# GpSimd's constants and half batch 1's decay rows issued earlier, and the planner's keys reset, in a fused forgetting attention and gated FFN

## The chip, the cores and the metric

The kernel runs on one core of a Trainium2 chip. A time is the device time of one execution in microseconds (us); lower is better. Before the change the median of five runs is 271.87 us (271.43 to 272.63). The profile is one execution, taken by the hardware profiler. Its engines are PE (TensorE matmul), PEld (TensorE weight load), DVE (VectorE), ACT (ScalarE), POOL (GpSimd) and SP (SyncE, which here only issues DMAs). A name with a q (SPq) is the queue of that engine.

## The reference

Eight batches, eight heads, 576 positions, head dimension 64. Attention has a decay: the logs of the forget gates f are summed along the sequence, and the difference of the sums is added to the scaled score. The outcome, eight heads side by side, is the input of an FFN: a matmul to 1024 channels, ReLU, a convolution over three neighbouring positions, a sigmoid gate, and a matmul back to 512.

```python
cum = cumsum(log(clip(f, 1e-4, 1)), -1)
s = q @ k.T / 8 + cum[..., :, None] - cum[..., None, :]      # causal
x = softmax(s) @ v                                            # heads side by side: (8, 576, 512)
h = maximum(x @ w_in, 0)
c = cw[0] * h[t - 1] + cw[1] * h[t] + cw[2] * h[t + 1]        # zero outside the sequence
out = (h * sigmoid(c)) @ w_out
```

## The kernel before

**Attention.** The work goes in 16 half batches `hb` of four heads, each in two pairs `i` of two heads. q and k of a half batch come by transposing DMAs on SP's queue (`load_qk`, L110) as 16-bit halves of their fp32 numbers into `stq` and `stk`, 128 rows by 4 x 576 columns, in a ring of four buffers each. Of the rows that hold low halves, some carry other things: rows 126 of `stq` and 96 and 98 of `stk` carry the decay sums as a high and a low bfloat16 part (`khi`, `klo`). Before use, DVE multiplies a buffer by a 0/1 column and adds another (`clamp`, L119), and POOL writes constant rows into it by DMA (`fill`, L132, from the tile `consts`, which DVE fills in L544 to L546). From half batch `CLAMPS` on, the query side has no DVE clamp, but a fill of 48 rows more. Decay rows come for half batch 0 from the small tiles `khi4` and `klo4` (`rows_first(p, eng)`, pair by pair, L125 to L127), for half batch 1 from `khi_sb` and `klo_sb` (`rows_of`, L140 to L142), and for the others from `kd`, a copy in DRAM that L253 and L254 write (L144, L146).

Scores of a pair are a diagonal part (L330 lays down the causal mask, L298 adds q and k), two off-diagonal parts (L298), and, once per half batch, the tail of 64 positions (L304). ACT takes their exp (L338, L324, L310). PV (`pv`, L356) multiplies with V, which five DMAs on SP load per half batch (L163; per whole batch from half batch `HALVES` on) and DVE casts to fp16 (L170 to L173). It writes the one PSUM tile `O`; `norm` (L367, L369, DVE) reads it, divides by the row sums into `xn` and so frees it for the next pair's PV. w_in is loaded by POOL in one DMA (L634), which waits for a DVE write behind the norm of pair 0.

**FFN.** When a batch's four pairs are normed, PE transposes `xn` (L393, L401), ACT or DVE copies it out (L411, L413), and L425 multiplies with w_in: 16 groups of four matmuls per batch. ACT does ReLU (L438), DVE the convolution in two instructions (L455, L457), ACT tanh (L467; sigmoid in the last batch, L465), DVE the gate (L475, L473), PE the last matmul (L487, L500), ACT or DVE the copy out (L511, L513), POOL or SP the store (L520, L522). The weights of the convolution are transposed and prepared once (L275 to L287).

**The order.** Each engine works through its instructions in order. Up to L269 the order is that of the text: clamps and decay sums of half batch 0 on DVE, a few matmuls to keep PE running (L241), the first loads, the constants. After that it is made by a planner: `task(engines, after, key, fn, ...)` notes a cost per engine, what comes ahead of it, and a key; `play` (L713) runs the tasks in a list schedule with these costs, where an engine that is free takes the ready task with the lowest key, and the instructions are issued in that order. `t_norm` is the norm, the clamps are tasks of the key `2 * hb - 3 + 0.2 * s`, `AHEAD` bounds how far scores may run ahead of the FFN, `busy` says when each engine is thought to be free first.

## Time and profile before

| | before |
|---|---|
| median of 5 runs | 271.87 us |
| profiled execution | 272.01 us |
| its span, first to last instruction | 270.1 us |
| mean granted TensorE clock | 0.974 |
| PE busy | 240.8 us, 89% |
| DVE busy | 226.3 us, 84% |
| ACT busy | 212.0 us, 79% |
| POOL busy | 59.1 us, 22% |
| DMA queue of SP | 32.00 MB, 70.1% of 16 engines' span |

Busy time is the time in which an instruction of the engine runs; issuing a DMA counts for POOL alone. In a line of the timeline or of the waits, the first two numbers are start and length in us; then come engine, line, operation, what is written and what is read; the bracket at the end tells how long the engine stood idle before, and what ended that. In the chain of waits each piece was released by the one above it, back from the end of the kernel. The time to landing of a DMA counts from its issue.

### The profile page before, as it was taken

The page shows a single profiled execution, that of the slowest core. Times are in us where ns is not written, and L with a number is a line of the kernel's source. Part 1 is how long each engine was busy: PE and PEld are TensorE (multiplying, and loading weights), DVE is VectorE, ACT ScalarE, POOL GpSimd, SP SyncE. Part 2 cuts the span into 40 slices and gives each one's busy share as a digit, 9 for nine tenths or more (in the row PEclk, how much of TensorE's full clock was granted, in tenths as well). Part 3 has the DMA queues.
Part 4 walks back from the last instruction along what each step waited for, and adds up shares of the span by engine and source line. Part 5 has one row for each costly group of instructions (what it writes and reads, how often), then busy time and mean ns, then how long its engine had stood idle before and what let it go on. Part 6 is the DMA issues. An engine that isn't in the chain of part 4 may idle for free.

```text
span 270.1 us, 6596 instructions
## 1 busy us (share of the span) xinstructions
PE 240.8 (89%) x2577; PEld 166.2 (62%) x2602; DVE 226.3 (84%) x401; ACT 212.0 (79%) x347; POOL 59.1 (22%) x124
## 2 busy tenths in 40 slices
PE   2966779876999999999999999999999999989990
PEld 1335646655777777676776677667776767654640
DVE  4864548999799999999989989999899999978751
ACT  5081738889879999989989899989999998577552
POOL 4391111821131240314315050404110100000000
PEclk9995979999999999999999999999999999999997
DMA  7999999999999999999999999999411201022015
GB/s 130 219 219 185 222 184 236 190 186 208 188 225 176 211 238 197 209 233 223 263 211 180 222 269 182 190 138 233 127 43 37 80 0 67 14 117 80 0 47 226
DMA packets 121284, 44.58 MB, mean 165 GB/s; under 512 B 115560, under 2 KB 116596, under 8 KB 121254
## 3 DMA queue, kind: packets, MB, share of 16 engines
q1 hardware_dynamic: 115088, 32.00, 70.1%
q0 software_dynamic: 5840, 12.01, 17.2%
q8 instruction: 20, 0.33, 0.6%
q10 hardware_dynamic: 326, 0.17, 0.4%
q14 instruction: 10, 0.08, 0.1%
HBM read 13.99 MB, written 9.58 MB: 87 GB/s over the span
## 4 chain that ended last, share of the span: by engine, by line
PE 65%; DMA 10%; SPq 8%; issue 5%; ACT 5%; DVE 4%; POOL 0%; ACTq 0%; POOLq 0%
PE mm L425 19%; PE mm L487 19%; PE sc L298 12%; PE O L356 8%; DMA stk<-in_k_dram 6%; SPq L110 6%; DMA vf<-in_v_dram 3%; SPq L163 2%; PE sc L330 2%; PE sc L500 2%; PE mm L393 2%; DVE u L457 1%; DMA out_dram<-ob 1%; ACT po L324 1%; ACT ht L438 1%
## 5 line engine op out<-in xcount | busy, mean ns | idle before, releaser
L425 PE MATMUL mm<-xt,w_in_f 128*128 128x288 f16 x512 | 80.0, 290 | 1.8 <-DVE xt L413 0.4
L298 PE MATMUL sc<-stq,stk 128*128 128x128 bf16 (+3 forms) x576 | 67.2, 242 | 7.5 <-ACT pm L338 4.0
L324 ACT ACTIVATE po<-sc 128x1024 f16<-128x1024 f32 x64 | 64.6, 1028 | 2.0 <-PE sc L298 1.5
L438 ACT ACTIVATE ht<-mm 128x288 f16<-128x288 f32 x128 | 52.0, 414 | 11.9 <-PE mm L425 10.8
L425 PEld LDWEIGHTS <-w_in_f 128*128 128x128 f16 x512 | 47.8, 99 | 18.8 <-issue 3.5
L487 PE MATMUL mm<-w_out_f,hg 128*128 128x512 f16 x248 | 58.4, 379 | 0.7 <-ACT xt L411 0.6
L298 PEld LDWEIGHTS <-stk 128*128 128x128 bf16 x576 | 42.4, 99 | 27.0 <-issue 8.1
L455 DVE SCALAR_TENSOR_TENSOR u<-ht,cwt 128x576 f32<-128x576 f16 x64 | 51.5, 812 | 5.5 <-ACT ht L438 4.7
L457 DVE SCALAR_TENSOR_TENSOR u<-ht,cwt,u 128x576 f32<-128x576 f16 x64 | 51.6, 812 | 0.5
L475 DVE SCALAR_TENSOR_TENSOR hg<-hg,ht 128x576 f16<-128x576 f16 x56 | 41.7, 752 | 4.1 <-ACT hg L467 3.7
L467 ACT ACTIVATE hg<-u,cwt 128x576 f16<-128x576 f32 x56 | 43.4, 780 | 1.4 <-DVE u L457 1.3
L338 ACT ACTIVATE pm<-sc 128x1024 f16<-128x1024 f32 x32 | 32.9, 1027 | 12.2 <-DVE consts L544 6.1
L487 PEld LDWEIGHTS <-hg 128*128 128x128 f16 x248 | 23.6, 98 | 24.2 <-issue 0.9
L356 PE MATMUL O<-va,po 128*128 128x65 f16 x640 | 37.1, 195 | 1.2 <-ACT po L324 1.0
L356 PE MATMUL O<-va,pm 128*128 128x65 f16 x256 | 31.6, 195 | 3.2 <-DVE xn L369 1.8
L356 PEld LDWEIGHTS <-po 128*128 128x128 f16 x640 | 31.1, 98 | 2.4 <-ACT po L324 1.8
L132 POOL DMA_DIRECT2D stq<-consts x23 | 12.9, 563 | 76.6 <-DMA stq<-in_q_dram 26.9
L356 PEld LDWEIGHTS <-pm 128*128 128x128 f16 x256 | 24.4, 99 | 6.0 <-DVE xn L369 2.7
L369 DVE TENSOR_TENSOR xn<-O,rc 128x640 f16<-128x640 f32 x32 | 26.4, 824 | 1.1
L511 ACT ACTIVATE ob<-mm 128x512 f32<-128x512 f32 x23 | 13.7, 598 | 11.0 <-PE mm L487 10.7
L330 PE MATMUL sc<-trib,identb 128*128 128x512 bf16 x39 | 15.0, 385 | 1.3 <-ACT po L324 1.3
L522 POOL DMA_DIRECT2D out_dram<-ob x10 | 7.5, 750 | 39.5 <-ACT ob L511 20.2
(112 smaller groups left out, 223.0 us busy)
## 6 DMA issues: line engine op xcount, KB each, us to landing
vf<-in_v_dram SPq DMA_DIRECT2D x64, 128.0 KB, 3.8
out_dram<-ob POOLq DMA_DIRECT2D x10, 512.0 KB, 5.4
out_dram<-ob SPq DMA_DIRECT2D x10, 256.0 KB, 2.1
stq<-consts POOLq DMA_DIRECT2D x8, 216.0 KB, 4.6
vf<-in_v_dram SPq DMA_DIRECT2D x16, 64.0 KB, 5.2
w_in_f<-in_moe_w_in_dram POOLq DMA_DIRECT2D x1, 1024.0 KB, 9.9
w_out_f<-in_moe_w_out_dram POOLq DMA_DIRECT2D x4, 256.0 KB, 6.1
out_dram<-ob SPq DMA_DIRECT2D x2, 512.0 KB, 2.8
```

The costliest lines, as they stand in the source:

```text
L298: nc.tensor.matmul(sc, stk_t[hb % RING][:, k0:k0 + 128], stq_t[hb % RING][:, q0:q0 + w], start=start, stop=stop, skip_group_check=True)
L324: nc.scalar.activation(p_of[i, s][:, 0:1024], sc_of.pop((i, s)), AF.Exp, scale=SCALE)
L338: nc.scalar.activation(p_of[i, 2], sc_of.pop((i, 2)), AF.Exp, scale=SCALE)
L356: nc.tensor.matmul(O[:, s, 65 * Q:65 * (Q + 1)], w, va[:, h, m, :], start=(m == 0), stop=(m == Q))
L369: nc.vector.tensor_tensor(xo, Ov[:, :, :, 0:64], rc.unsqueeze(3).broadcast_to((128, 2, NKB, 64)), op=ALU.mult)
L425: nc.tensor.matmul(ps[:, 0:w], w_in_f16[:, cc, 128 * ff:128 * (ff + 1)], xt[:, cc, w * t:w * (t + 1)], start=(cc == 0), stop=(cc == NCC - 1))
L438: nc.scalar.activation(ht[:, 0, HT_0 + w * t:HT_0 + w * (t + 1)], ps[:, 0:w], AF.Relu)
L455: nc.vector.scalar_tensor_tensor(u, hl, cwt[:, ff, 0:1], hc, op0=ALU.mult, op1=ALU.add)
L457: nc.vector.scalar_tensor_tensor(u, hr, cwt[:, ff, 1:2], u, op0=ALU.mult, op1=ALU.add)
L467: nc.scalar.activation(hv, u, AF.Tanh, scale=cwt[:, ff, 2:3])
L475: nc.vector.scalar_tensor_tensor(hv, hv, 1.0, hc, op0=ALU.add, op1=ALU.mult)
L487: nc.tensor.matmul(ps, chunk(g, ff, c), w_out_f16[:, ff, :], start=(ff == 0), stop=(ff == NFF - 1))
```

## The change

The memsets of POOL (ones and zeros around V and around the hidden tile, and the identity) stand before the loads of half batch 1's q and k in the text, and so ahead of POOL's first row DMAs. The rows of both pairs of half batch 0 are issued on ACT's queue. Half batch 1's rows are two tasks: the query row with the query transposes as its condition, the key rows with those of the keys. The copies to `kd` are a task behind them, on which the rows of the later half batches depend. Beside that, numbers of the planner are different: `CLAMPS` 6 in place of 8, `HALVES` 8 in place of 16, `AHEAD` 5.0 in place of 3.0, POOL's first free time, the keys of casts, norms, the second convolution and the copies out, and a few costs. The instructions of the program are as many as before on PE; on DVE two query clamps fewer.

```diff
@@ -119,12 +119,12 @@
         nc.vector.tensor_scalar(t, t, lim[0:p1, 2 * side:2 * side + 1], lim[0:p1, 2 * side + 1:2 * side + 2],
                                 op0=ALU.mult, op1=ALU.add)
 
-    def rows_first(p, eng):
+    def rows_first(p):
 
         tq, tk, c, r = stq_t[0], stk_t[0], slice(2 * p * S, 2 * (p + 1) * S), slice(64 * p, 64 * (p + 1))
-        eng.dma_start(tq[126:127, c], khi4[r, :])
-        eng.dma_start(tk[96:97, c], khi4[r, :])
-        eng.dma_start(tk[98:99, c], klo4[r, :])
+        nc.scalar.dma_start(tq[126:127, c], khi4[r, :])
+        nc.scalar.dma_start(tk[96:97, c], khi4[r, :])
+        nc.scalar.dma_start(tk[98:99, c], klo4[r, :])
 
     def fill(t, p0, n, z):
 
@@ -132,16 +132,18 @@
         nc.gpsimd.dma_start(bass.AP(tensor=t.tensor, offset=int(t.offset) + p0 * row, ap=[[2 * row, n], [1, HS]]),
                             consts[z:z + n, :])
 
+    def row_q(hb, decay):
+        nc.gpsimd.dma_start(stq_t[hb % RING][126:127, 0:HS], decay)
+
+    def rows_second():
+
+        for p, t in ((96, khi_sb), (98, klo_sb)):
+            nc.gpsimd.dma_start(stk_t[1][p:p + 1, 0:HS], t[HH:2 * HH, :])
+
     def rows_of(hb):
 
-        tq, tk = stq_t[hb % RING], stk_t[hb % RING]
-        c = slice(hb * HH, (hb + 1) * HH)
-        if hb == 1:
-            nc.gpsimd.dma_start(tk[96:97, 0:HS], khi_sb[c, :])
-            nc.gpsimd.dma_start(tk[98:99, 0:HS], klo_sb[c, :])
-            nc.gpsimd.dma_start(tq[126:127, 0:HS], khi_sb[c, :])
-            return
-        nc.gpsimd.dma_start(tq[126:127, 0:HS], kd[0:1, c, :].rearrange("j h s -> j (h s)"))
+        c, tk = slice(hb * HH, (hb + 1) * HH), stk_t[hb % RING]
+        row_q(hb, kd[0:1, c, :].rearrange("j h s -> j (h s)"))
         row = HS + 64
         nc.gpsimd.dma_start(bass.AP(tensor=tk.tensor, offset=int(tk.offset) + 96 * row, ap=[[2 * row, 2], [1, HS]]),
                             kd[:, c, :].rearrange("j h s -> j (h s)"))
@@ -232,32 +234,6 @@
     nc.vector.tensor_scalar(cum4, cum4, off4, float(-1.0 / SCALE), op0=ALU.add, op1=ALU.mult)
     nc.vector.tensor_copy(khi4, cum4)
     nc.vector.tensor_tensor(klo4, cum4, khi4, op=ALU.subtract)
-    load_qk(1, 0, 4)
-    for side in range(2):
-        clamp(0, side, 0, 2)
-    rows_first(0, nc.scalar)
-
-    for t in range(16):
-        nc.tensor.matmul(ops, identb, trib, start=True, stop=True)
-
-    nc.vector.tensor_tensor_scan(cum, one1[0:BH].broadcast_to((BH, S)), fsb, 0.0, op0=ALU.mult, op1=ALU.add)
-    nc.vector.tensor_scalar(khi_sb, cum, float(-1.0 / SCALE), None, op0=ALU.mult)
-    nc.vector.scalar_tensor_tensor(klo_sb, cum, float(-1.0 / SCALE), khi_sb,
-                                   op0=ALU.mult, op1=ALU.subtract)
-    for side in range(2):
-        clamp(0, side, 2, 2)
-    rows_first(1, nc.gpsimd)
-    nc.vector.memset(vf_t[0][0:1, 0, 0, 0:1], 0.0)
-    load_v(0, 0, HH)
-    load_v(0, HH, H)
-    nc.gpsimd.dma_start(kd[0], khi_sb)
-    nc.gpsimd.dma_start(kd[1], klo_sb)
-    for t in range(RING):
-        nc.vector.memset(stk_t[t][:, HS:HS + 64], 0.0)
-    for t in range(2):
-        nc.vector.memset(p4_t[t][:, HH * SL:], 0.0)
-    for t in range(4):
-        nc.vector.memset(po_t[t][:, 1024:], 0.0)
     for t in range(3):
         nc.gpsimd.memset(va_t[t][64:128, :, NKB - 1, :], 0.0)
         nc.gpsimd.memset(va_t[t][:, :, 0:NKB - 1, 64:65], 1.0)
@@ -267,6 +243,30 @@
     for t in range(NHT):
         nc.gpsimd.memset(ht_t[t][:, :, 0:HT_0], 0.0)
         nc.gpsimd.memset(ht_t[t][:, :, HT_0 + S:HT_W], 0.0)
+    load_qk(1, 0, 4)
+    for side in range(2):
+        clamp(0, side, 0, 2)
+    rows_first(0)
+
+    for t in range(16):
+        nc.tensor.matmul(ops, identb, trib, start=True, stop=True)
+
+    nc.vector.tensor_tensor_scan(cum, one1[0:BH].broadcast_to((BH, S)), fsb, 0.0, op0=ALU.mult, op1=ALU.add)
+    nc.vector.tensor_scalar(khi_sb, cum, float(-1.0 / SCALE), None, op0=ALU.mult)
+    nc.vector.scalar_tensor_tensor(klo_sb, cum, float(-1.0 / SCALE), khi_sb,
+                                   op0=ALU.mult, op1=ALU.subtract)
+    for side in range(2):
+        clamp(0, side, 2, 2)
+    rows_first(1)
+    nc.vector.memset(vf_t[0][0:1, 0, 0, 0:1], 0.0)
+    load_v(0, 0, HH)
+    load_v(0, HH, H)
+    for t in range(RING):
+        nc.vector.memset(stk_t[t][:, HS:HS + 64], 0.0)
+    for t in range(2):
+        nc.vector.memset(p4_t[t][:, HH * SL:], 0.0)
+    for t in range(4):
+        nc.vector.memset(po_t[t][:, 1024:], 0.0)
 
 
     def conv_weights():
@@ -545,17 +545,22 @@
         nc.vector.memset(z[0:2, :], PAIR)
         nc.vector.memset(z[32:33, :], MINUS)
 
-    CLAMPS, HALVES, LANDING = 8, 16, 3.0
+    CLAMPS, HALVES, LANDING = 6, 8, 3.0
     HELD, POOLED = 4, 4
     WAITS = ((3, 0), (3, 1), (4, 0), (4, 1))
     room = {"sc": 2, "O": 1, "mm": 2, "pm": 2, "xn": 2, "xt": 2, "u": 2, "ht": NHT,
             "hg": 2, "ob": 3}
     t_load, t_v, t_rows, t_va, t_qk, t_pv, t_norm, t_xt = {}, {}, {}, {}, {}, {}, {}, {}
-    t_gate, t_cast, t_xt0, t_wout = {}, {}, {}, []
+    t_gate, t_cast, t_xt0, t_even, t_wout = {}, {}, {}, {}, []
     t_ident = task({"SP": 0.01}, [], -9, lambda: None, lag=9.0)
     t_cw = task({"PE": 1.0}, [t_ident], 2.9, conv_weights, take="mm", give=[("mm", 1)], lag=2.0)
 
     last = None
+
+    def copy_decay():
+        nc.gpsimd.dma_start(kd[0], khi_sb)
+        nc.gpsimd.dma_start(kd[1], klo_sb)
+
     t_fsrc = task({"DVE": 3.1}, [], -9, fill_sources)
     for hb in range(NHB):
         key = 2 * hb - 5.5
@@ -589,18 +594,19 @@
         elif hb % 2 == 0:
             last = t_v[b] = task({"SP": 3.5}, [t_cast[2 * b - j, p] for j in (4, 3) for p in range(2)] if b >= 2 else [],
                                  key + 1.2, lambda b=b: load_v(b), lag=2.3, dma=6.0, behind=last)
-        for j, (h, side) in enumerate(WAITS):
-            if h == hb:
-                x = task({"DVE": 0.1}, [even[1] if side == 0 else even[-1]], -9, lambda j=j: hold(w_out_f16[:, 2 * j:2 * j + 2, :]))
-                t_wout.append(task({"POOL": 0.8}, [x], 2 * hb - 1.0, lambda j=j: load_w_out(j), lag=2.0, dma=1.7))
+        t_even[hb] = even
         if hb:
-            t_rows[hb] = even + [task({"POOL": 1.1 if hb > 1 else 1.6}, landed, 2 * hb - 3.6 if hb > 1 else -9 if hb > 1 else -1.0,
-                                      lambda hb=hb: rows_of(hb), lag=LANDING + 1.0)]
+            if hb == 1:
+                t_rows[hb] = even + [task({"POOL": 0.55}, landed[0:1], -9, lambda: row_q(1, khi_sb[HH:2 * HH, :]), lag=4.0),
+                                     task({"POOL": 1.1}, landed[1:2], -9, rows_second, lag=4.0)]
+                t_kd = task({"POOL": 1.3}, [t_rows[hb][-1]], -1.0, copy_decay, lag=4.0)
+            else:
+                t_rows[hb] = even + [task({"POOL": 1.1}, landed + [t_kd], 2 * hb - 3.6, lambda hb=hb: rows_of(hb), lag=LANDING + 1.0)]
         else:
             t_rows[hb] = []
         for p in range(2):
             t_cast[hb, p] = task({"DVE": 0.75 if p == 0 else 0.42},
-                                 [t_half or t_v[b]] + ([t_pv[2 * hb - 5, 1]] if hb >= 3 else []), 2 * hb - 1.1 + 0.5 * p,
+                                 [t_half or t_v[b]] + ([t_pv[2 * hb - 5, 1]] if hb >= 3 else []), 2 * hb - 2.1 + 0.5 * p,
                                  lambda hb=hb, p=p: cast_v(hb, p, nc.vector), lag=0.2)
 
         for p in range(2):
@@ -608,7 +614,7 @@
             if i == 1:
                 t_rows[hb] = [t_second]
             if p == 0:
-                x = t_second = task({"ACT": 0.01}, [], -9, lambda: None, lag=3.7) if i == 0 else None
+                x = t_second = task({"ACT": 0.01}, [], -9, lambda: None, lag=2.3) if i == 0 else None
                 t_tail = x = task({"PE": 0.36}, t_rows[hb] + [x] * (i == 0), i + (0.02 if i else 0.65),
                                   lambda hb=hb: tail_scores(hb), take="sc")
                 tail = task({"ACT": 0.36}, [x] + ([t_pv[i - 3, 1]] if hb >= 2 else []), i + 0.02,
@@ -628,7 +634,7 @@
                                   + ([t_pv[i, 0]] if s else []), i + 0.9 + 0.4 * s,
                                   lambda i=i, s=s: pv(i, s), take="O" if s == 0 else None,
                                   give=[("pm", mask)] if s else [])
-            t_norm[i] = task({"DVE": 1.05}, [t_pv[i, 1]], i - 0.0, lambda i=i: norm(i) if i else [norm(i), hold(w_in_f16)],
+            t_norm[i] = task({"DVE": 1.05}, [t_pv[i, 1]], i - 1.0, lambda i=i: norm(i) if i else [norm(i), hold(w_in_f16)],
                              take="xn" if i % PPB == 0 else None, give=[("O", t_pv[i, 0])])
             if i == 0:
                 t_win = task({"POOL": 1.0}, [t_norm[0]], -0.5, lambda: nc.gpsimd.dma_start(
@@ -636,12 +642,18 @@
         if hb % 2:
             early, late = [t_norm[i - 3], t_norm[i - 2]], [t_norm[i - 1], t_norm[i]]
             t_xt0[b] = x = task({"PE": 0.46}, early, i - 0.7, lambda b=b: xpose_pe(b, 0), take="mm", also="xt")
-            t_xt[b] = [task({"DVE": 0.75, "ACT": 1.05}, [x], i - 1.0, lambda e, b=b: xpose_out(b, 0, 0, e), give=[("mm", x)])]
+            t_xt[b] = [task({"DVE": 0.7, "ACT": 1.05}, [x], i - 1.0, lambda e, b=b: xpose_out(b, 0, 0, e), give=[("mm", x)])]
             x = task({"PE": 0.46}, late + [t_xt0[b]], i + 0.3, lambda b=b: xpose_pe(b, 2), take="mm")
             t_xt[b].append(task({"DVE": 0.75, "ACT": 1.05}, [x], i, lambda e, b=b: xpose_out(b, 2, 2, e), give=[("mm", x)]))
             x = task({"PE": 0.25}, late, i + 0.35, lambda b=b: xpose_tail(b), take="mm",
                      give=[("xn", t_norm[i - 3])], behind=x)
             t_xt[b].append(task({"DVE": 0.3, "ACT": 0.4}, [x], i, lambda e, b=b: xpose_out(b, "t", 0, e), give=[("mm", x)]))
+
+
+    for j, (h, what) in enumerate(WAITS):
+        x = t_norm[h] if what == 2 else t_even[h][-1 if what else 1]
+        x = task({"DVE": 0.1}, [x], -9, lambda j=j: hold(w_out_f16[:, 2 * j:2 * j + 2, :]))
+        t_wout.append(task({"POOL": 0.8}, [x], h if what == 2 else 2 * h - 1.0, lambda j=j: load_w_out(j), lag=2.0, dma=1.7))
 
 
     start = [PPB * (b0 + nb) + 1.0 for b0, nb in GROUPS]
@@ -664,7 +676,7 @@
                                   lambda g=g, ff=ff, t=t: relu(g, ff, t),
                                   give=[("mm", x)]))
             y = task({"DVE": 0.23 + n / 1020.0}, relus + [t_cw], key + 0.15, lambda g=g, ff=ff: conv(g, ff, 0), take="u")
-            x = task({"DVE": 0.23 + n / 1020.0}, [y], key + 0.14, lambda g=g, ff=ff: conv(g, ff, 1))
+            x = task({"DVE": 0.23 + n / 1020.0}, [y], key + 0.5, lambda g=g, ff=ff: conv(g, ff, 1))
             x = task({"ACT": 0.19 + n / 1200.0 + (1.3 if (g, ff) == (LAST, 0) else 0.0)},
                      [x] + (t_tanh[0:1] or t_exp), key - 0.5, lambda g=g, ff=ff: tanh(g, ff),
                      give=[("u", y)], take="hg" if ff == 0 and g % 2 == 0 else None)
@@ -697,7 +709,7 @@
                 if late:
                     t_late.append(x)
             t_m2.append(x)
-            x = task({"DVE": 0.62, "ACT": 0.57}, [x] + ([y] if c % 2 else []), key - 1.0,
+            x = task({"DVE": 0.62, "ACT": 0.57}, [x] + ([y] if c % 2 else []), key - 0.0,
                      lambda e, g=g, c=c: evac(g, c, e), give=[("mm", x)] if g < LAST else [], take="ob" if c % 2 == 0 else None)
             single = c == 8 or g >= LAST - 1
             if c % 2 or single:
@@ -708,10 +720,10 @@
         if g % 2:
             task({"SP": 0.01}, t_m2, key, lambda: None, give=[("hg", t_hg)])
 
-    AHEAD, QUEUED = 3.0, 8.0
+    AHEAD, QUEUED = 5.0, 8.0
 
     def play():
-        busy = {"PE": 11.5, "ACT": 12.0, "DVE": 12.0, "POOL": 14.0, "SP": 19.0}
+        busy = {"PE": 11.5, "ACT": 12.0, "DVE": 12.0, "POOL": 12.4, "SP": 19.0}
         ready = {e: [] for e in busy}
         dma_free, clock = 21.5, 0.0
         heap, order = [], []
```

## The prediction, before the changed kernel was run

> **What bounds the kernel now.** I read the table of windows first, to see in which stretch an engine sets the pace.
>
> ```profile
> 42.20:56.06 13.86, 11.88 (x149) 8.90 (x149) 13.21 (x25) 12.63 (x22) 5.59 (x9) 1.00 1.17 204
> 56.06:78.00 21.94, 18.23 (x253) 13.44 (x253) 19.49 (x36) 18.38 (x28) 5.79 (x10) 1.00 1.25 203
> 78.00:235.00 157.00, 155.18 (x1753) 110.90 (x1773) 147.50 (x238) 141.50 (x237) 32.42 (x57) 1.00 0.89 165
> ```
>
> The columns are window, length, busy time of PE, PEld, DVE, ACT and POOL, granted clock, DMA share, GB/s. From 78 to 235 us PE is busy 155.18 of 157.00: it is the bound, only 1.82 us can be won there, and whatever start-up delays is kept to the end. From 42 to 56 DVE is busy 13.21 of 13.86, so there DVE leads. Start-up is where this change acts, so I read the chain of waits next.
>
> ```profile
> 23.48 10.68 DMA stk<-in_k_dram
> 34.19 0.88 DVE stk L119
> 35.23 0.83 DVE xn L369
> 36.54 1.02 ACT xt L411
> 37.61 4.67 PE mm L425 x22
> ```
>
> Half batch 2's keys are issued at 23.48 and land at 34.17. DVE then clamps them, norms pair 3, ACT copies the transposed x, and the first FFN matmuls run at 37.61. Why the keys take 10.7 us is in the timeline and the DMA issues:
>
> ```profile
> 21.27 0.80 POOL L634 DMA_DIRECT2D w_in_f<-in_moe_w_in_dram  x1 [1.01 <-DVE w_in_f L151]
> 23.48 7.54 SPq L110 DMA_TRANSPOSE stk<-in_k_dram  x1
> w_in_f<-in_moe_w_in_dram POOLq DMA_DIRECT2D x1, 1024.0 KB, 9.9
> stk<-in_k_dram SPq DMA_TRANSPOSE x1, 10.7
> ```
>
> w_in (1 MB) is in flight from 21.27 to 31.2, across the key transposes; the five other key transposes up to 50 us land in 4.2 to 6.2 us. Last, PE and DVE around the places that the change touches:
>
> ```profile
> 18.22 0.43 DVE L170 TENSOR_SCALAR va<-vf 128x512 f16<-128x512 f32 x1 [1.03 <-DMA vf<-in_v_dram]
> 24.27 0.37 PE L298 MATMUL sc<-stq,stk 128*128 128x64 bf16 x4 [1.21 <-DMA stq<-khi_sb]
> 32.22 0.21 DVE L367 RECIPROCAL rc<-O 128x10 f32<-128x10 f32 x1
> 33.34 0.20 PE L356 MATMUL O<-va,pm 128*128 128x65 f16 x1 [1.36 <-DVE xn L369]
> 34.19 0.88 DVE L119 TENSOR_SCALAR stk<-stk,lim 96x2304 uint16<-96x2304 uint16 x1 [0.91 <-DMA stk<-in_k_dram]
> 34.98 0.21 DVE L367 RECIPROCAL rc<-O 128x10 f32<-128x10 f32 x1
> 36.11 0.40 PE L393 MATMUL mm<-ident,xn 128*128 128x128 f16 x4 [1.42 <-DVE xn L369]
> ```
>
> PE loses 1.21 us to half batch 1's decay rows; that is what the change goes for. And norm of pair 2 (32.22) runs before the key clamp (34.19), so that DVE waits 0.91 us for the keys with only pair 3's norm behind it.
>
> **The change part by part.**
> *First pairs' rows on ScalarE's queue.* Three issues of 0.70, 0.56 and 0.53 leave POOL; ScalarE's own three of that kind took 0.52, 0.49 and 0.61. They can start at 11.0 (clamps end at 10.71 and 11.20) and end near 12.7; behind them on ScalarE stands its first exp, at 12.84. Landing 3.1 to 3.4 us after a start near 12.1, the last row is there at 15.3 instead of 15.54, against a PE wait that ended at 15.70. It gains 0.3 us on pair 1's scores, or loses 0.2 if the issues run over the first exp. Neither counts: PV of pair 0 waits for V (18.22 above), the exps end at 19.71, PV of pair 1 starts at 21.01. Without that cover it would be -0.3 to +0.2. I take 0.
>
> *Constants earlier.* The memsets and ident took POOL from 13.84 to 17.54, 3.7 us; they move into its idle 7.02 us before 11.01. Hidden on POOL. On DVE the bounds are 0 and one longest POOL operation (0.72 us, the ident cast) in the way of a DVE operation before the first scores; the same 1.3 us between 19.71 and 21.01 covers that. The nearest rows are DVE's clamps at 15.50 and 16.33, which ran beside the ident operations and took 0.90 and 0.86, against 0.87 alone at 31.43. I take 0. The Trainium skill (SBUF — State Buffer, Who interferes with whom) says that VectorE's two-port operations and GpSimd's exclude each other for a whole instruction, which speaks against moving them beside the decay. By that rule a few such hits would add 1 to 2 us before the first scores, of which up to 0.7 us would show; the two clamps above show no such hit.
>
> *Half batch 1's rows.* The source constants are ready when DVE ends them, at 15.47, as before. POOL is now free by then: the query row can go at 12.8 (transposes issued 7.87, landing 4.9), then fill 0.55, two key rows 0.54 and 0.50, fill 0.67, ending near 17.8 instead of 20.26. Landing 3.8 to 4.8 us after issue, all are there by 22. Behind them the two kd copies (0.53 each) end near 18.9; next on POOL is w_in, which waits for pair 0's norm until 21.27, and kd's first reader is at 28.82. PE's order still has PV of pair 1 ahead, ending at 22.8, so the wait of 1.21 goes and no more: -1.2 us for half batch 1, 0 at worst.
>
> *VectorE's order.* The changed program issues the key clamp of half batch 2 ahead of the norm of pair 2; before, it stood between the norms of pairs 2 and 3. DVE works in order, so everything behind waits for the keys. What decides when they land is not touched: w_in is issued after pair 0's norm, which is bound by V, and SP's order is the same. So I leave 34.17. Without this, pair 2's norm would start at 32.22 - 1.2 = 31.0; with it, at 34.98, where pair 3's started before. Pair 2's norm ends 1.07 later (36.05), PV of pair 3 takes 1.19 more from there (33.28 to 34.47 before: 37.24), pair 3's norm 1.07 (38.3, and 36.05 before), then 1.56 to the FFN as before: 39.9 instead of 37.61, +2.3. That is at full clock. PE would stand from 30.7 (31.9 less 1.2) to 36.1, 5.4 us at a stretch. Before, 3.4 us at half clock followed idle times of 1.36 and 1.42:
>
> ```profile
> 20.50:27.50 7.00, 5.06 (x54) 4.14 (x56) 2.46 (x7) 1.44 (x3) 0.80 (x1) 0.51 1.21 185
> 34.20:37.60 3.40, 1.51 (x23) 0.99 (x20) 2.11 (x4) 1.01 (x1) 1.02 (x2) 1.00 1.22 125
> 37.60:41.00 3.40, 3.39 (x15) 2.09 (x15) 1.13 (x2) 1.24 (x3) 0.00 (x0) 0.51 1.22 259
> ```
>
> At half clock PV of pair 3 takes 0.7 more (1.84 at 21.01, 1.13 at 33.34) and the transposes 0.3: 40.9, +3.3. The Trainium skill (TensorE: Matmul & The Clock Gate, What's actually happening) has the clock fall after an idle window of some 3.4 us and rise after a busy one. By that rule the long stall falls in the half-clock end, +3.3.
>
> The new order puts 16 FFN matmuls before half batch 2's scores, not 24 (0.49 per four, so 0.98 of work left for later). Full clock: scores at 39.9 + 1.96 = 41.9 against 42.28, and PE is 0.6 behind in work. Half clock: 40.9 + 3.9 = 44.8, and PE is 3.5 behind. DVE's first convolution (39.77) is late by 2.3 to 3.3. I take 2.9 for both, near the half-clock end, since PE's idle time grows where before already ended in a half clock.
>
> *What is given back.* Between 42.2 and 78 DVE has 3.1 us idle (0.65 and 2.45) and PE 5.7. The same work stands ahead of half batch 5's scores in both orders, so the delay can shrink by DVE's idle time at most: kept 0 to 2.9. Most of that idle time is an in-order wait for the other engine, so I take 0.9 back and keep 2.0.
>
> *The rest.* Two query clamps (half batches 6 and 7, 0.87 each) leave DVE for two more fills on POOL, which has the time (32.42 of 157 busy); DVE is not the bound there: 0. V in whole batches from half batch 8: SP waits for PE in that stretch, 0. The many swaps of norm, convolution and output copy between 78 and 235: gain at most 1.82; if a stretch of 20 us (about a batch) fell to the 83% of the 56-78 row, a loss of 3.1. Most swaps are local and an order at 98.8% has little to give: 0. From the last batch's tail transposes on, all engines keep their order: 0.
>
> Sum: +2.0. The profiled execution took 272.01 (span 270.1 and 1.9 around it), 0.14 over the median, 271.87. So **273.9 us**.
>
> **The rivals.**
> *The keys land early (faster).* With five rows out of the way, the keys' transfer gets ahead of w_in. If they land by 30.1, the clamp is done before pair 2's norm is due and the 1.2 us stay: 270.7. Break-even is where 5.7 us from landing to FFN (34.17 to 39.9) ends at 37.61, a landing at 31.9. For it: normal landings of 4 to 6 us. Against it: the rows are a few KB, and w_in is issued at 21.27 still.
> *Absorbed (same).* The delay is real, but DVE's 3.1 us idle take nearly all of 2.9: about 272.2. Against it: from 42 to 56 DVE has 0.65 idle.
> *A worse order later (slower still).* On top of the 2.0, a batch of the steady stretch loses 3.1: 277.0. For it: with 6% idle on DVE, a convolution put behind a norm makes PE wait. Against: PE idles 1.82 us in 157 now, and the swaps leave each batch's set of operations as it is.
>
> **How the numbers follow.** My forecast holds 0.52 (its own range 272.8 to 275.4), keys early 0.20, absorbed 0.14, worse order 0.14. A measurement here can tell about 0.3%, 0.8 us, from no change. The range goes into the early-keys case (270.6) and into the worse order (276.3). Faster takes the early keys, 0.21 with a little of the absorbed; same is the rest of that, 0.13; slower 0.66.
>
> **What would show it.** Right: in the changed profile DVE's clamp of half batch 2's keys waits several us for the DMA; pair 2's norm starts near 35; PE stands some 5 us before PV of pair 3; the first FFN matmul comes near 40 or later; the wait on half batch 1's row is gone; from 78 to 235 PE stays near 98.8%. Wrong: keys landing before 32, a clamp that waits under 2 us, or a 56-78 stretch with PE over 90% busy.

## The result, and the profile after

The changed kernel takes 273.87 us (median of 37 runs, 271.44 to 280.56) against 272.2 for the kernel before on the same chips (63 runs, 271.09 to 276.53). The ratio is 1.0041 with a 95% interval of 1.0025 to 1.0056: slower by about 1.1 us, as forecast in sign, and within 0.1 us of the forecast 273.9 in the median. But the profile shows another way to that number than the one forecast. (Ratios here leave out executions that ran at a disturbed clock, medians don't; that is why a ratio can be nearer to 1 than two medians.) The profiled execution took 275.32 (span 273.4), 1.45 over its own median, so of the 3.3 us between the two profiled spans only a part is typical.

The timeline of ScalarE in the changed kernel (columns: start, duration, engine, line, operation, tiles, and the idle time before it with its releaser):

```profile
15.37 0.47 ACTq L125 DMA_DIRECT2D stq<-khi  x1
16.22 0.48 ACTq L126 DMA_DIRECT2D stk<-khi  x1
18.09 0.47 ACTq L127 DMA_DIRECT2D stk<-klo  x1
18.61 1.02 ACT L338 ACTIVATE pm<-sc 128x1024 f16<-128x1024 f32 x1 [12.56 <-DMA stq<-khi]
```

The three row transfers of pair 1 are issued at 15.37, 16.22 and 18.09, not at 11.0 to 12.7, though their sources and the clamps are done by 11.0. ScalarE works in order, so the first exp stands behind them: 18.61 instead of 12.84. TensorE, GpSimd, SyncE and VectorE after that, from their timelines:

```profile
19.68 1.01 PE L298 MATMUL sc<-stq,stk 128*128 128x448 bf16 x4 [6.47 <-ACT pm L338]
22.36 0.32 PE L298 MATMUL sc<-stq,stk 128*128 128x64 bf16 x3 [1.31 <-DMA stk<-klo]
37.70 0.20 PE L356 MATMUL O<-va,pm 128*128 128x65 f16 x1 [1.36 <-DVE xn L369]
42.24 4.02 PE L425 MATMUL mm<-xt,w_in_f 128*128 128x288 f16 x16 [1.31 <-DMA w_in_f<-in_moe_w_in_dram]
```

```profile
22.32 2.53 SPq L110 DMA_TRANSPOSE stk<-in_k_dram  x1
28.74 0.86 POOL L640 DMA_DIRECT2D w_in_f<-in_moe_w_in_dram  x1 [10.01 <-DVE w_in_f L153]
35.78 0.87 DVE L119 TENSOR_SCALAR stk<-stk,lim 96x2304 uint16<-96x2304 uint16 x1
36.57 0.21 DVE L367 RECIPROCAL rc<-O 128x10 f32<-128x10 f32 x1
```

TensorE waits 6.47 us for the first exp. Pair 0's norm moves from 19.87 to 27.34, and with it w_in, which waits for that norm: issued at 28.74 instead of 21.27. That has a good side and a bad one. Half batch 2's keys, issued at 22.32, no longer share the DMA engines with w_in; they land near 26.9, after 4.6 us instead of 10.7, and VectorE's clamp of them (35.78) waits for no transfer, although it does stand ahead of pair 2's norm (36.57). But w_in itself is now last, as the chain of waits of the changed kernel says (columns: start, duration, piece):

```profile
10.36 4.93 DMA stk<-in_k_dram
...
18.73 10.00 issue
...
28.74 13.46 DMA w_in_f<-in_moe_w_in_dram
...
42.24 4.02 PE mm L425 x16
```

The 10.00 us of `issue` are GpSimd standing ahead of w_in; the line of L640 above names the write behind pair 0's norm as what ended them. The first FFN product starts at 42.24; in the same timeline of the kernel before it starts at 37.11 (the prediction's 37.61 is where its chain of waits enters these products). Later the gap closes a little: half batch 2's tail scores come 3.95 us later than before (46.06 for 42.11), half batch 3's 3.1 (59.17 for 56.06), half batch 15's 3.6 (217.94 for 214.31), the end 3.3. The windows of the changed kernel at two places (columns as in the prediction):

```profile
12.00:20.00 8.00, 1.53 (x14) 0.92 (x15) 5.30 (x8) 1.39 (x2) 4.40 (x7) 0.74 1.09 213
...
80.00:237.00 157.00, 155.75 (x1762) 111.17 (x1781) 145.77 (x239) 139.31 (x238) 33.99 (x59) 1.00 0.86 167
```

From 12 to 20 us TensorE works 1.53 of 8.00 us (5.44 before). From 80 to 237 it works 155.75 of 157.00, and the same from 78 to 235, the prediction's window, where the kernel before has 155.18: 0.57 us more. The transposes of the batches' tails (L401) say much the same: those of batch 1 come 4.04 us later than before (72.78 for 68.74), those of the last batch 3.68 later (239.57 for 235.89). So in this one profile the new order gains some 0.4 to 0.6 us in the steady stretch.

Why are the rows issued so late? The list of ScalarE's instructions in the changed program shows what each waits for:

```
L125 DMACopy stq0<-khi4  [waits DMAHW1, DVE]
L126 DMACopy stk0<-khi4  [waits DMAHW2, DVE]
L127 DMACopy stk0<-klo4  [waits DMAHW4]
L125 DMACopy stq0<-khi4  [waits DMAHW0, DVE]
L126 DMACopy stk0<-khi4  [waits DMAHW3, DVE]
L127 DMACopy stk0<-klo4  [waits DMAHW6]
L338 Activation pm<-sc   [waits PE]
```

DMAHW0 to DMAHW7 are the completion semaphores of transfers from SyncE's and ScalarE's queues. The program uses eight, in turn, so each transfer waits until the one eight places ahead of it, on either engine, has landed. For pair 0's rows (the first three) those had landed long before. For pair 1's they are half batch 1's key transposes (DMAHW0, issued 10.36, landing 15.29 by the chain above), V's first transfer (DMAHW3, landing at 16.2) and V's third (DMAHW6, landing at 18.1). The rows are issued at 15.37, 16.22 and 18.09, each right behind its landing. None of these three transfers has anything to do with the rows.

### The profile page after: what moved, and what is told of

Its sections match the earlier page's. It is cut to its first block, busy times and chain, and to the rows that moved or that the text cites. A ratio compares the mean times of both kernels' runs of the same rounds, so it can differ in the third digit from the quotient of the medians.

```text
span 273.4 us, 6553 instructions
## 1 busy us (share of the span) xinstructions
PE 240.7 (88%) x2576; PEld 165.6 (61%) x2602; DVE 224.5 (82%) x400; ACT 209.3 (77%) x346; POOL 58.4 (21%) x123
## 4 chain that ended last, share of the span: by engine, by line
PE 69%; DMA 8%; DVE 6%; issue 6%; ACT 5%; SPq 3%; POOL 1%; ACTq 0%; POOLq 0%
PE mm L425 20%; PE mm L487 19%; PE sc L298 13%; PE O L356 9%; DMA w_in_f<-in_moe_w_in_dram 5%; SPq L110 3%; PE sc L330 2%; PE sc L500 2%; DMA stk<-in_k_dram 2%; PE mm L393 2%; DVE u L455 1%; DVE xn L369 1%; DVE u L457 1%; DVE hg L475 1%; ACT ht L438 1%
## 5 line engine op out<-in xcount | busy, mean ns | idle before, releaser
L425 PE MATMUL mm<-xt,w_in_f 128*128 128x288 f16 x512 | 80.3, 291 | 2.0 <-DMA w_in_f<-in_moe_w_in_dram 1.3
L298 PE MATMUL sc<-stq,stk 128*128 128x128 bf16 (+3 forms) x576 | 67.2, 244 | 12.7 <-ACT pm L338 7.9
L324 ACT ACTIVATE po<-sc 128x1024 f16<-128x1024 f32 x64 | 65.3, 1029 | 2.3 <-PE sc L298 2.1
L425 PEld LDWEIGHTS <-w_in_f 128*128 128x128 f16 x512 | 47.6, 99 | 18.6 <-issue 1.6
L356 PEld LDWEIGHTS <-po 128*128 128x128 f16 x640 | 30.4, 97 | 2.1 <-ACT po L324 1.2
L511 ACT ACTIVATE ob<-mm 128x512 f32<-128x512 f32 x28 | 16.7, 598 | 11.0 <-PE mm L487 10.8
L367 DVE RECIPROCAL rc<-O 128x10 f32<-128x10 f32 x32 | 7.0, 218 | 14.0 <-PE O L356 13.7
```

Source lines behind the costliest of these rows:

```text
L298: nc.tensor.matmul(sc, stk_t[hb % RING][:, k0:k0 + 128], stq_t[hb % RING][:, q0:q0 + w], start=start, stop=stop, skip_group_check=True)
L324: nc.scalar.activation(p_of[i, s][:, 0:1024], sc_of.pop((i, s)), AF.Exp, scale=SCALE)
L356: nc.tensor.matmul(O[:, s, 65 * Q:65 * (Q + 1)], w, va[:, h, m, :], start=(m == 0), stop=(m == Q))
L425: nc.tensor.matmul(ps[:, 0:w], w_in_f16[:, cc, 128 * ff:128 * (ff + 1)], xt[:, cc, w * t:w * (t + 1)], start=(cc == 0), stop=(cc == NCC - 1))
```

## The experiments

The theories, as they were named before the runs. **L**: ScalarE's queue is held by those reused semaphores, and the first exp behind it. **K**: the forecast's, VectorE's clamp of half batch 2's keys ahead of pair 2's norm waits for keys that land near 34. **N**, **P** and **R** came up later: N, the planner's new numbers cost; P, the early rows of half batch 1 cost nothing on the chip, but the order that the planner makes when they stand in its list does; R, the early rows themselves cost. "Old numbers" are the planner's constants and keys in the kernel before, "new numbers" those of the changed kernel.

**1. Pair 1's rows back on GpSimd's queue, all else as changed.**

```diff
-    def rows_first(p):
+    def rows_first(p, eng):
...
-    rows_first(1)
+    rows_first(1, nc.gpsimd)
```

> The changed kernel with the rows of pair 1 back on GpSimd's queue; all else, VectorE's order included, is the changed kernel's. Theory L (ScalarE's queue: its rows of pair 1 stand 15.37 to 18.56 because each waits for the completion semaphore of a transfer eight places earlier, and the first exp stands behind them): the first exp starts at 12.8 to 13.1 instead of 18.61, TensorE's wait of 6.47 us at 19.68 is gone, w_in is issued near 21.3 and the keys of half batch 2 land near 34 again, as in the kernel before. Theory K (the forecast's: VectorE's clamp of half batch 2's keys ahead of pair 2's norm): in that state the clamp waits over 2 us for the keys, PV of pair 3 starts near 39 and the first FFN product at 40 to 41. L and K: about 2 us over the kernel before, near 274. L without K: up to 1.2 us below it, near 271.

273.82 us, ratio 1.0041 (1.0019 to 1.0063): the same as the changed kernel. From the timelines of VectorE and TensorE of this run:

```profile
35.41 0.88 DVE L119 TENSOR_SCALAR stk<-stk,lim 96x2304 uint16<-96x2304 uint16 x1 [3.91 <-DMA stk<-in_k_dram]
36.21 0.21 DVE L367 RECIPROCAL rc<-O 128x10 f32<-128x10 f32 x1
...
37.33 0.23 PE L356 MATMUL O<-va,pm 128*128 128x65 f16 x1 [6.62 <-DVE xn L369]
41.65 3.74 PE L425 MATMUL mm<-xt,w_in_f 128*128 128x288 f16 x16 [0.38 <-DVE xt L413]
```

The first exp is back at 13.96 and w_in at 22.01, so L's part is gone. In its place stands the forecast's picture, row by row: keys late (24.52, landing near 35.4), VectorE's clamp waiting 3.91 us, TensorE standing 6.62 us before PV of pair 3, the FFN at 41.65. Two different waits lead to nearly the same late FFN; taking one away uncovers the other. (The profiled execution took 279.59, 5.8 over the median. Its extra time lies behind these lines: at 72.68 TensorE waits 5.25 us for a fill of constant rows.)

**2. The kernel before, with only pair 1's rows on ScalarE's queue.**

```diff
-    rows_first(1, nc.gpsimd)
+    rows_first(1, nc.scalar)
```

> The kernel before with one edit: the three row transfers of pair 1 on ScalarE's queue. Theory L: ScalarE issues them at about 15.4, 16.2 and 18.1 and the first exp starts at about 18.6 instead of 12.84; w_in is issued near 28.7 and lands near 42, the first FFN product starts near 42 instead of 37.61; the time is 1 to 4 us over the kernel before. Theory K (only VectorE's order costs): issues at 11.0 to 12.7, first exp at 12.9, no difference of over 0.3%.

274.47 us, ratio 1.0048 (1.0015 to 1.008). ScalarE's timeline repeats that of the changed kernel:

```profile
15.59 0.48 ACTq L125 DMA_DIRECT2D stq<-khi  x1
16.36 0.47 ACTq L126 DMA_DIRECT2D stk<-khi  x1
18.28 0.47 ACTq L127 DMA_DIRECT2D stk<-klo  x1
18.80 1.02 ACT L338 ACTIVATE pm<-sc 128x1024 f16<-128x1024 f32 x1 [12.49 <-DMA stk<-khi]
```

So L is enough by itself for about 1.3 us (0.48% of 272). The FFN starts at 40.39, not at 42: w_in, issued at 28.12, was in time here.

**3. Experiment 1, with the clamp of half batch 2's keys made to follow pair 2's norm.**

```diff
-  even.append(task({"DVE": 0.9}, [x], ...
+  even.append(task({"DVE": 0.9}, [x] + ([t_norm[2]] if hb == 2 and s else []), ...
```

> The first experiment, and the clamp of half batch 2's keys made to follow pair 2's norm, as in the kernel before. Theory K: 2 to 3 us faster than the first experiment, 270.5 to 271.5, since norm of pair 2 no longer waits for keys that land near 34; the first FFN product at about 37. Theory L alone: the same as the first experiment within 0.3%.

The FFN starts at 37.77, 3.9 us earlier than in experiment 1, and yet the run is no faster: 274.87 us, ratio 1.0073 (1.0044 to 1.0102). K is right about the place and wrong about what it is worth in this list: the 3.9 us are lost again later. In its profile (276.81, 1.9 over the median) half batch 3's tail scores come 1.04 us earlier than before (55.02 for 56.06) and batch 1's tail transposes 4.72 later (73.46 for 68.74), so most of the loss falls between 55 and 74 us. That neither L nor K could explain, and led to experiments 5 to 9.

**4. The changed kernel, all rows on ScalarE's queue; only the write that holds V's transfers back moves behind them.**

```diff
-    nc.vector.memset(vf_t[0][0:1, 0, 0, 0:1], 0.0)
+    nc.scalar.copy(vf_t[0][0:1, 0, 0, 0:1], one1[0:1, 0:1])
```

With it V's transfers come after the rows in the program, and the rows of pair 1 get DMAHW4, 5 and 6, last used by transfers that are long done.

> The changed kernel with all rows on ScalarE's queue as they are; only the one-element write that holds the V transfers back moves from VectorE to ScalarE, behind the six rows, so that the V transfers come after the rows in the program and take other completion semaphores: the rows of pair 1 then reuse those of transfers that landed before 10.5. Theory L: the rows are issued at 10.9 to 13.0 and the first exp starts at 12.9 to 13.3, though the same transfers are on the same queue; the V transfers now wait in SyncE's queue for half batch 1's keys (15.3), so half batch 2's transposes are issued 1 to 2 us later than in the first experiment; the time is 1 to 3 us below the changed kernel if its first FFN product starts before 41. A rival, that ScalarE's queue itself or the rows' data are late: issues at 15 to 18 again and no gain.

```profile
10.95 0.47 ACTq L125 DMA_DIRECT2D stq<-khi  x1
11.52 0.56 ACTq L126 DMA_DIRECT2D stk<-khi  x1
12.12 0.61 ACTq L127 DMA_DIRECT2D stk<-klo  x1
14.01 1.02 ACT L338 ACTIVATE pm<-sc 128x1024 f16<-128x1024 f32 x1 [1.05 <-PE sc L298]
...
36.42 0.88 DVE L119 TENSOR_SCALAR stk<-stk,lim 96x2304 uint16<-96x2304 uint16 x1 [3.79 <-DMA stk<-in_k_dram]
```

Same queue, same transfers, other semaphores: issued at 10.95 to 12.12, and the first exp waits for TensorE alone. That shows L's mechanism. The time is worse, against what was expected: 276.8 us, ratio 1.0138 (1.01 to 1.0176). As in experiment 1 the keys' wait is back (3.79), on top of V's transfers, which now wait on SyncE for half batch 1's keys; the FFN starts at 42.66. (The profiled execution took 280.80, 4.0 over the median; a wait of 3.30 us at 72.36 stands behind these lines.)

**5. The kernel before, with GpSimd's constants early and nothing else** (the block of memsets and the identity moved to where the diff of the change has it).

> The kernel before with GpSimd's constants written while VectorE prepares the decay, and nothing else; every engine's order is otherwise that of before. The forecast's step for this part was 0: the constants end near 7.6 instead of 18, GpSimd's row transfers of pair 1 stay near 11.0, the first FFN product stays at 37 to 38, and the time is that of before within 0.3%. A rival, that the writes on GpSimd slow VectorE's decay: first exp over 0.3 us later than 12.84.

272.29 us, ratio 1.0004 (0.9986 to 1.0021): no difference. TensorE's timeline:

```profile
36.53 0.59 PE L393 MATMUL mm<-ident,xn 128*128 128x128 f16 x4 [3.53 <-DVE xn L369]
37.83 2.43 PE L425 MATMUL mm<-xt,w_in_f 128*128 128x288 f16 x10 [0.38 <-DVE xt L413]
```

With GpSimd free earlier the wait for half batch 1's rows (1.21 us at 24.27 before) is already gone in this run, and nothing is won: TensorE gets to the transposes sooner and waits 3.53 us there, where it waited 1.42, because the keys still land near 34.6. The first exp came at 13.84, 1.0 later than before, as the rival said, but not for the rival's reason: VectorE ended the decay (klo) at 6.10, and at 6.39 before. In experiment 2, where the constants stand in their old place, the first scores were as late (13.30, behind 2.83 us of waiting for the klo row). Why those rows land late in some runs isn't shown.

**6. Experiment 5, and half batch 1's rows early as in the change; old numbers, pair 1's rows on GpSimd's queue.**

```diff
+            if hb == 1:
+                t_rows[hb] = even + [task({"POOL": 0.55}, landed[0:1], -9, lambda: row_q(1, khi_sb[HH:2 * HH, :]), lag=4.0),
+                                     task({"POOL": 1.1}, landed[1:2], -9, rows_second, lag=4.0)]
+                t_kd = task({"POOL": 1.3}, [t_rows[hb][-1]], -1.0, copy_decay, lag=4.0)
```

> The fifth experiment, and half batch 1's rows issued as its keys land, the decay's copy behind them; rows of pair 1 on GpSimd's queue, the planner's numbers those of before. The planner then places the clamp of half batch 2's keys ahead of pair 2's norm, as in the changed kernel. Theory K (that order costs while the keys land near 34): VectorE's clamp waits over 2 us, the first FFN product at 40 to 42, 0.7 to 2 us over the kernel before. Theory N (the planner's new numbers cost, not the order): within 0.3% of before, though the FFN starts late.

279.51 us, ratio 1.0262 (1.022 to 1.0304): 7 us slower, far over the expected 0.7 to 2. The clamp of the keys waits 4.21 us and the FFN starts at 41.30, as K has it; but half batch 3's tail scores are only 2.6 us later than in the kernel before (58.64 for 56.06). The larger part is lost far behind the start. The windows over the first 20 of the last 40 us of the span, and TensorE's timeline there:

```profile
238.80:248.80 10.00, 8.17 (x48) 4.67 (x48) 7.69 (x11) 7.48 (x14) 0.00 (x0) 1.00 0.20 79
248.80:258.80 10.00, 9.39 (x42) 4.52 (x42) 4.71 (x8) 4.54 (x11) 0.00 (x0) 0.83 0.08 28
```

```profile
249.34 2.87 PE L487 MATMUL mm<-w_out_f,hg 128*128 128x512 f16 x8 [1.74 <-ACT ht L438]
```

**7. Experiment 6, with the clamp behind pair 2's norm** (the edit of experiment 3).

> The sixth experiment, and the clamp of half batch 2's keys made to follow pair 2's norm. Theory K: the first FFN product at 36.5 to 38 and the time 0.5 to 1.5 us below the sixth experiment, at before's or up to 1.2 us under it (TensorE's wait of 1.21 us at 24.27 gone). Theory N: also at or under before, and so about 2 us below the third experiment, which has the same order here and the new numbers. If it stands 1 to 2 us over before all the same, neither the clamp's place nor the planner's numbers, but the early rows themselves (or what is late behind them after 44 us) cost.

277.43 us, ratio 1.0164 (1.0125 to 1.0203). Here K's order is worth 0.98% of 272.4, 2.7 us; with the new numbers it was worth nothing (1 to 3). Still 1.6% over before, so K is not the main cause, and N falls: the old numbers are not better with these rows.

**8. The changed kernel with the old numbers.**

```diff
-    CLAMPS, HALVES, LANDING = 6, 8, 3.0
+    CLAMPS, HALVES, LANDING = 8, 16, 3.0
...
-    AHEAD, QUEUED = 5.0, 8.0
+    AHEAD, QUEUED = 3.0, 8.0
```

(and the keys, lags and POOL cost of the change set back likewise)

> The changed kernel with the planner's numbers of before; rows on ScalarE's queue, constants early and half batch 1's rows early as in the changed kernel. Theory L: rows of pair 1 issued at about 15.4, 16.2 and 18.1 as there, first exp near 18.6, first FFN product at 40 to 42.5, 0.5 to 2 us over the kernel before. Theory N: more than 0.3% below the changed kernel's 273.9.

280.07 us, ratio 1.0251 (1.02 to 1.0303). The rows of pair 1 are late again (15.52 to 18.34, first exp 18.86), the FFN starts at 41.82, and the time is that of experiment 6. So ScalarE's queue costs nothing extra where the keys' wait would come anyway, as between the changed kernel and experiment 1.

**9. Early constants and early rows on the chip, but not in the planner's list.** The rows of half batch 1 are written inside the tasks that fill its other rows; the decay's copy takes the place of the old row task. TensorE, VectorE, ScalarE and SyncE run exactly the order of the kernel before.

```diff
-                                 lambda t=t, rows=rows: [fill(t, *x) for x in rows],
+                                 lambda hb=hb, s=s, t=t, rows=rows: [second(s) if hb == 1 else None] + [fill(t, *x) for x in rows],
```

> Constants early and half batch 1's rows early, as in the sixth experiment, but the planner's list is that of the kernel before: the rows are written inside the tasks that fill half batch 1's other rows, and the decay's copy takes the place of the old row task. TensorE's, VectorE's, ScalarE's and SyncE's orders are exactly those of before; only GpSimd's queue differs. Theory P (the early rows cost nothing by themselves; what costs 7 us in the sixth experiment is the order that the planner makes of them, on all engines): first FFN product at 36.5 to 38.5, time within 0.3% of before, 6 to 8 us below the sixth. Theory R (the early rows cost, by what they collide with on the DMA rings): 1 us or more over before.

272.61 us, ratio 1.001 (0.9986 to 1.0033). P holds, R falls: the same rows at the same early place (the key rows at 16.86 and 17.57, in experiment 6 at 16.85 and 17.60) cost nothing, and gain nothing. At the same distance from the end as in experiment 6 the windows read:

```profile
231.90:241.90 10.00, 8.94 (x72) 5.36 (x70) 8.63 (x13) 6.55 (x12) 0.00 (x0) 1.00 0.14 53
241.90:251.90 10.00, 9.57 (x57) 5.28 (x55) 8.07 (x12) 7.70 (x14) 0.00 (x0) 1.00 0.21 80
```

TensorE is busy 18.51 us of these 20 at full clock; in experiment 6 it is busy 17.56, and at 0.83 of the clock in the second ten. Experiment 6's half batch 2 tail scores come 1.4 us later than here (45.10 for 43.66), half batch 3's 1.0 (58.64 for 57.60), half batch 15's 3.25 (219.41 for 216.16), and its end 6.9 later (span 278.8 for 271.9).

**10. Experiment 5, with w_in in two halves.**

```diff
+        nc.gpsimd.dma_start(w_in_f16[:, :, 512 * j:512 * (j + 1)],
+                            moe_w_in.rearrange("(cc p) ff -> p cc ff", p=128)[:, :, 512 * j:512 * (j + 1)])
```

> The fifth experiment with w_in loaded in two halves of 512 KB: the first where all of it was issued (near 21.5), the second after the rows of half batch 2's keys (near 35); all other engines' orders as before. If the 1 MB of w_in is what holds half batch 2's keys until 34, they land at 29 to 32 and SyncE's later loads move up with them; the first FFN product starts at 35.5 to 37 and the time is 0.3 to 2 us under before. If the keys' landing is set by the other transfers, they land at 33 to 35 and the time stays within 0.3%.

```profile
32.80 0.87 DVE L119 TENSOR_SCALAR stk<-stk,lim 96x2304 uint16<-96x2304 uint16 x1
36.45 4.39 PE L432 MATMUL mm<-xt,w_in_f 128*128 128x288 f16 x24 [0.38 <-DVE xt L420]
```

The keys are there before the clamp at 32.80, which no longer waits, and the FFN starts at 36.45 (L432 is L425 of the other kernels): w_in does hold the keys back. The ratio is 0.9978 (0.9955 to 1.0001), a gain of 0.2% that the interval does not settle.

**11. Experiments 9 and 10 together.**

> The ninth and the tenth experiment together, as a candidate that beats both kernels: the sum of both, 270 to 272.5 us.

275.61 us, ratio 1.011 (1.0069 to 1.0151): not the sum of the two, a miss. In its profile the FFN starts at 36.06, and then TensorE stands for 10.81 us before half batch 3's tail scores, whose keys SyncE takes 12.62 us to issue:

```profile
37.79 12.62 SPq L110 DMA_TRANSPOSE stk<-in_k_dram  x1
50.67 0.37 PE L307 MATMUL sc<-stq,stk 128*128 128x64 bf16 x4 [10.81 <-issue]
```

The second half of w_in (issued 34.18) runs into the next half batch's transposes; the profiled execution took 282.33 and is the longest of this kernel, so the whole stall is not typical. What makes the other executions 1.1% longer isn't shown.

**12. Experiment 9 with the new numbers.**

> The ninth experiment with the changed kernel's planner numbers: early rows on the chip, no early rows in the planner's list, rows of pair 1 on GpSimd's queue. With it the four of old and new numbers, with and without the rows in the list, are complete (fifth or ninth, sixth, first, this). If the new numbers pay only for the listed rows, this stands 1 to 4 us over before; if they are better by themselves, at or under before; if they cost by themselves what the first experiment lost, about 273.8.

The four executions spread from 275.44 to 280.64, ratio 1.0114 (1.0064 to 1.0163), which rests on the two shortest. With it the four cases with pair 1's rows on GpSimd's queue are complete (the first two lines):

| ratio to the kernel before | half batch 1's rows not in the list | in the list |
|---|---|---|
| old numbers | 1.0010 (exp. 9) | 1.0262 (exp. 6) |
| new numbers | 1.0114 (exp. 12) | 1.0041 (exp. 1) |
| old numbers, rows of pair 1 on ScalarE | 1.0048 (exp. 2, constants as before) | 1.0251 (exp. 8) |
| new numbers, rows of pair 1 on ScalarE | not run | 1.0041 (the change) |

The list costs 2.5% with the old numbers; the new numbers cost 1.0% alone and win back 2.2% with the list. Neither of the two, or both together, stays within 0.4% of the kernel before; each alone costs more, and none of the four is under it.

## Why the prediction was right or wrong

**First pairs' rows on ScalarE's queue, taken as 0: this step failed.** It read the clamps' ends (10.71 and 11.20) as the only thing that the issues wait for, and gave 11.0 to 12.7. They came at 15.37 to 18.09 and the first exp at 18.61, not 12.84, because each reused a completion semaphore of a transfer still in flight (changed kernel, experiments 2 and 4). In the old list that costs 1.3 us (experiment 2). The Trainium skill (DMA: Bandwidth & Descriptors, Issuing engines are not separate DMA queues) says that issuing from several engines only saves the sequencer's time for the issue, usually small; here it saved GpSimd 1.8 us that nothing needed, and made ScalarE's first exp 5.8 us late.

**"So I leave 34.17": failed with it.** The forecast held that nothing touches the keys' landing since w_in is issued after pair 0's norm. That norm moved from 19.87 to 27.34 with the exp, w_in from 21.27 to 28.74, and the keys landed near 26.9. So the signs listed as right (a clamp waiting several us, TensorE standing some 5 us before PV of pair 3) are not in the changed profile, and the sign listed as wrong, keys before 32, is. Norm of pair 2 near 35 (36.57) and an FFN at 40 or later (42.24) were there for another reason. The rival "keys land early" met its condition, a landing before 30.1, and still did not give its 270.7: w_in took the keys' place as the last to land, which it had not priced.

**VectorE's order, +2.9: the mechanism is real, hidden behind the other.** Experiment 1 shows it with each row that the forecast named: clamp waiting 3.91 us, norm at 36.21 (34.98 forecast), TensorE standing 6.62 us (5.4), FFN at 41.65 (39.9 to 40.9). Its value in time depends on the list: 2.7 us between experiments 6 and 7, none between 1 and 3.

**Constants earlier, 0: right** (experiment 5, 1.0004). The rule of the Trainium skill weighed there (SBUF — State Buffer, Who interferes with whom), that VectorE's two-port operations and GpSimd's exclude each other, shows as little more than nothing in the changed kernel: the cast of khi took 0.35 us beside a GpSimd memset (5.57), 0.18 before. That is 0.17 us, not 1 to 2, and the decay still ended earlier than before (6.13 for 6.39). The scan of 128x18 took 0.38 for 0.18 too, but beside GpSimd's copy of trit (3.57 to 4.28), which the change does not touch.

**Half batch 1's rows, -1.2: the wait went, the gain did not come.** The wait of 1.21 us is gone in the changed kernel and in experiments 5 and 9; the last two are at 1.0004 and 1.001. What is late next is what the forecast's own chain had shown, half batch 2's keys: TensorE's wait before the transposes grew from 1.42 to 3.53 us in experiment 5. The term should have been 0. The forecast's total did not hold it: its FFN was worked out from the keys' landing alone.

**What is given back, 0.9.** In the profiled pair 5.1 us at the FFN became 3.1 at half batch 3's tail scores and 3.3 at the end. Part of the first drop is only the order: 16 FFN products stand ahead of half batch 2's scores, not 24. The medians differ by 1.7 and the ratio says 1.1, so typical executions lose less than the profiled one; where they lose less isn't shown by one profile.

**The many swaps, taken as 0: near right for the change as a whole, and not for its parts.** The forecast bounded the reordering by 1.8 us gained and 3.1 lost, and the steady stretch of the changed kernel gained 0.4 to 0.6. But the list alone moved the time by 7 us (experiments 9 and 6), and the new numbers on top of it by 5.7 the other way (279.51 to 273.82). That these nearly cancel was not foreseen. Of the 6.9 us between experiments 6 and 9, 3.25 are there by half batch 15's tail scores and 3.65 come after them, where TensorE waits 1.74 us for ScalarE and its clock falls. "From the last batch's tail transposes on, all engines keep their order" is true of the change, and no guide to what a list without the new numbers does there.

So the total was right by luck: errors met. At the FFN the changed kernel was 5.1 us late and not 2.9, through ScalarE's queue and then w_in, not through VectorE's clamp; of that 3.3 was left at the end of the profiled execution and 1.1 in the ratio, where the forecast kept 2.0. Nor do the two early waits alone explain the 1.1: with both away (experiment 3, FFN 0.66 us later than before) the time is still 0.73% over. What the new order loses there is not traced further than the stretch from 55 to 74 us.

## What to carry to other kernels

Before a transfer is moved to an engine that also computes, look at everything that its issue waits for in the program, completion semaphores of unrelated transfers included, and at what stands behind it in that engine's order. A wait that is taken away gains only what the next-latest input allows: here two early landings, w_in and the keys, each kept the FFN late when the other was freed. Where a planner writes the order out, an edit to its list is an edit to every engine to the last microsecond: run it once with the list left alone (experiment 9) to tell the edit from the order.

## What the runs showed of the hardware that was not expected

- SyncE's and ScalarE's queues are tied through the completion semaphores that their transfers share: a 2.2 KB row on ScalarE stood 4.3 us past its inputs (11.04) until a key transpose on SyncE had landed (15.29, issue at 15.37), and two more stood until V's transfers had.
- The same 1 MB of w_in landed in 9.9 us when issued at 21.27 and in 13.46 at 28.74, and half batch 2's keys in 10.7 us beside it and in 4.6 ahead of it: which of them starts first decides who waits, and the FFN needs both.
- In the changed kernel the granted clock was 0.50 from 17 to 26 us, within and after TensorE's wait of 6.47 us (to 19.68), and 0.50 again from 40 to 46; between 26 and 40 no wait of TensorE was longer than 1.36 us (37.70). The Trainium skill (TensorE: Matmul & The Clock Gate, What's actually happening) has the clock fall after an idle window of about 3.4 us. The first fall came in a wait longer than that, though early in it (0.80 already over 14 to 17 us); the second came without one.
